# A kernel of local and full attention: Exp planned at another rate, LayerNorm scalars on other engines, final checks in another place

## The chip, the cores and the metric

The kernel runs on one core of one Trainium2 chip. The metric is the device time of one execution in microseconds (us), read as the median of several executions. The profile comes from one of these executions (for the kernel before, from a further one of 1501.95 us), with its own span and its own mean granted clock of TensorE. Engines are named as in the profile: PE is TensorE (PEld its weight loads), DVE VectorE, ACT ScalarE, POOL GpSimd, SP SyncE. A reading "L1481" is a line of the kernel. Before and after have different line numbers for the same code; where both matter, both are given.

## The reference

Four residual layers on a bf16 array x of 2048 rows and 512 columns: local attention A, full attention B, then A and B again with the same weights. Both have 32 heads of width 16. A lets each row look at 8 rows before it at a step of 2. B shares one key and one value head among all query heads.

```python
# cut to what matters
def _layernorm(x, eps=1e-5):
    return (x - mean(x)) / sqrt(var(x) + eps)

def _B_ref(x, wq, wk, wv, wo):            # S = 2048, H = 32, Dh = 16
    q = (x @ wq).reshape(B, S, H, Dh).transpose(0, 2, 1, 3)
    k, v = x @ wk, x @ wv
    p = softmax(einsum("bhqd,bkd->bhqk", q, k) * Dh ** -0.5)
    return merge_heads(einsum("bhqk,bkd->bhqd", p, v)) @ wo

x = A_x
x = x + _A_ref(_layernorm(x), A_wqkv, A_wo)
x = x + _B_ref(_layernorm(x), B_wq, B_wk, B_wv, B_wo)
x = x + _A_ref(_layernorm(x), A_wqkv, A_wo)      # the same two again
x = x + _B_ref(_layernorm(x), B_wq, B_wk, B_wv, B_wo)
```

B sets the time: two layers with 2048 x 2048 scores for 32 heads make 4096 tiles of 128 keys by 512 queries, and each needs an exponential.

## The kernel before

The program has a scheduler of its own. When the kernel is built, it plays all work through with a planned duration for each operation and fixes the order of instructions on each engine. On the chip the order is never changed: each engine takes its instructions in turn and waits on semaphores. The plan's constants (biases, priorities) were searched for a short plan.

A score tile takes one of two ways. Two tiles go through an Exp on ScalarE, or one tile goes through a copy on VectorE that writes an integer from which an integer addition (the "pass", on VectorE and on GpSimd) makes the bits of an exponential.

```python
# planned durations: the Exp of n tiles, in the scheduler
    def exp(self, s, _):
        ...
        t = 426.7 * n + 52                    # 905 ns for two tiles
        S.run("act", s, t)
        done = s + t + LAT["act"]
        ...

# what it emits
    def exp(self, key, slot, pt, n):          # ScalarE: two tiles
        self.chain("act", self.nc.scalar.activation(out=self.pt[pt][:, 0:n, :], in_=..., func=AF.Exp, scale=E_SCALE))
    def copy(self, bank, buf, r):             # VectorE: one tile
        self.chain("dve", self.nc.vector.tensor_scalar(out=self.t[buf][:, r, :].bitcast(I16), in0=self.dv[bank][:],
                                                       scalar1=-U_BIAS, scalar2=U_BIAS, op0=ALU.max, op1=ALU.add))
    def do_pass(self, e, buf, out, j, n, both):
        if e == "pool":                       # int32 add on GpSimd, 1.9 us
            ...
        else:                                 # int16 add on VectorE
            ...

# LayerNorm: statistics on VectorE, four small GpSimd operations, then four norms on whichever engine is free
        def scalars(op, some):
            g, x = nc.gpsimd, slice(some[0], some[-1] + 1)
            self.chain("pool", g.tensor_scalar_add(out=ve[:, x], in0=mv[:, x, 1], scalar1=EPS))
            self.chain("pool", g.tensor_tensor(out=rstd[:, x], in0=ve[:, x], in1=self.w.nhalf[:, x], op=ALU.pow))
            self.chain("pool", g.tensor_tensor(out=nmr[:, x], in0=mv[:, x, 0], in1=rstd[:, x], op=ALU.mult))
            self.chain("pool", g.tensor_scalar(out=nmr[:, x], in0=nmr[:, x], scalar1=-1.0, scalar2=None, op0=ALU.mult))
        ...
            def norm(op, i=i, xn=xn):
                if op.eng == "act":
                    k = nc.scalar.activation(out=xn.t[:], in_=src(i), func=AF.Identity, scale=rstd[:, i:i + 1],
                                             bias=nmr[:, i:i + 1])
                else:
                    k = self.pick(op).tensor_scalar(out=xn.t[:], in0=src(i), scalar1=rstd[:, i:i + 1],
                                                    scalar2=nmr[:, i:i + 1], op0=ALU.mult, op1=ALU.add)
            n = xn.used(sm.used(self.op({"act": 830.0, "dve": 690.0, "pool": 940.0}, 0, norm, [nm[i], *xn.prev],
                                        prio=322.6 + self.PRIO, port=("pool",))))
```

`port` names the engines for which the scheduler keeps an operation off the VectorE passes and GpSimd passes that run at that time.

At the end, VectorE compares all sums and reciprocals of the softmax with limits ("flags"), reduces them to a minimum, and a tiny matmul counts the partitions that passed.

## Time and profile before

| | before |
|---|---|
| median of 3 runs | 1503.88 us (1503.73 to 1510.52) |
| span of the profiled run, granted clock | 1500.2 us, 0.994 |
| busy PE, DVE, ACT, POOL | 95%, 89%, 96%, 60% |
| Exps, VectorE copies | 1359, 1378 |
| idle ACT, DVE | 63 us, 161 us |

Lines of a group read: line, engine, operation, output<-input with shapes, count | busy us, mean ns of one record | idle time of the engine just before them and what ended it. The prediction shows the lines that bear on the bound. Three more are needed later. The first is the page's chain of waits by engine: the work that ended last, followed back to what each step waited for, as shares of the span. The second is the table of 50 us windows, here the one from 150 to 200 us, where the loss will show (columns: length; busy us of PE, PEld, DVE, ACT, POOL with counts; clock; DMA share; GB/s). The third is the view of one tile, the normed rows, on VectorE (count: shortest/median/longest ns, first and last start):

```profile
ACT 45%; PE 42%; issue 7%; DVE 4%; POOL 1%; DMA 0%; ACTq 0%; POOLq 0%; DVEq 0%
```

```profile
150.00:200.00 50.00, 48.63 (x391) 15.61 (x393) 41.02 (x74) 45.98 (x55) 25.99 (x21) 1.00 0.11 22
```

### The profile page before, as it was taken

Reading aid. Unit: us, or ns where it says so; the run is one execution under the profiler, and the core shown is the slowest. Engines: PE = TensorE matmul, PEld = TensorE weight load, DVE = VectorE, ACT = ScalarE, POOL = GpSimd, SP = SyncE. Lnnn points to the kernel's source line nnn. Section 1 sums busy time; section 2 is a strip of 40 time slices with the busy share of each in tenths; the row PEclk is TensorE's granted clock in tenths of the full one; section 3 lists DMA queues with packets and bytes.
Section 4 is the critical chain, followed back from the end, with each engine's and each line's share of the span. In section 5 each row is a group of like instructions: output and inputs, shape, how many; then the busy total and the mean of one; then the engine's idle time right before and its main releaser. Section 6 shows DMA issues by size and latency. Waiting matters only on the chain.

```text
span 1500.2 us, 42220 instructions
## 1 busy us (share of the span) xinstructions
PE 1430.8 (95%) x17204; PEld 494.9 (33%) x17263; DVE 1339.5 (89%) x2301; ACT 1437.1 (96%) x1754; POOL 896.9 (60%) x741
## 2 busy tenths in 40 slices
PE   8899999999999999999999999999999999999996
PEld 4534343223422233222333224322222222222222
DVE  5787868998799978999789997899999999999997
ACT  6899999999999999999999999999999999999995
POOL 3745546565566656666575664757566656665664
PEclk9999999999999999999999999999999999999999
DMA  4010110011010020100201001001000000000000
GB/s 142 5 29 3 30 16 16 17 31 34 14 23 13 17 38 7 27 13 16 35 13 27 13 15 16 16 9 43 27 12 14 13 23 17 9 18 20 16 9 24
DMA packets 84114, 32.95 MB, mean 22 GB/s; under 512 B 71688, under 2 KB 77448, under 8 KB 83912
## 3 DMA queue, kind: packets, MB, share of 16 engines
q1 hardware_dynamic: 83048, 28.33, 8.8%
q8 instruction: 137, 2.24, 0.6%
q10 hardware_dynamic: 864, 1.84, 0.3%
q14 instruction: 65, 0.53, 0.1%
HBM read 13.53 MB, written 2.61 MB: 11 GB/s over the span
## 4 chain that ended last, share of the span: by engine, by line
ACT 45%; PE 42%; issue 7%; DVE 4%; POOL 1%; DMA 0%; ACTq 0%; POOLq 0%; DVEq 0%
ACT pt L1481 40%; PE o L1507 14%; PE st L1466 14%; PE y L1130 3%; ACT P L1353 2%; PE q L1130 2%; PE k L1130 2%; PE qb L1130 2%; DVE t L1485 2%; PE v L1297 1%; PE dv L1466 1%; ACT logs L1403 1%; ACT rec L1405 1%; PE st L1346 1%; DVE i L1495 1%
## 5 line engine op out<-in xcount | busy, mean ns | idle before, releaser
L1481 ACT ACTIVATE pt<-st 128x1024 bf16<-128x1024 f32 x1359 | 1271.8, 1168 | 16.9 <-PE o L1507 9.1
L1490 POOL TENSOR_TENSOR i<-t,off 128x1024 int32<-128x1024 int32 x345 | 656.2, 1904 | 488.1 <-DVE i L1495 332.7
L1485 DVE TENSOR_SCALAR t<-dv 128x512 int16<-128x512 f32 x1378 | 877.9, 683 | 51.3 <-PE dv L1466 41.5
L1466 PE MATMUL st<-QT,KAB 32*128 32x512 bf16 x1388 | 270.4, 381 | 13.4 <-ACT pt L1481 8.1
L1466 PE MATMUL st<-QT,region 32*128 32x512 bf16 x1330 | 259.1, 379 | 18.4 <-ACT pt L1481 13.9
L1507 PE MATMUL o<-pt,region 128*32 128x512 bf16 x1330 | 270.7, 386 | 0.2
L1507 PE MATMUL o<-i,region 128*32 128x512 f16 x1436 | 265.3, 385 | 1.0 <-DVE i L1495 0.7
L1507 PE MATMUL o<-pt,VEa 128*32 128x512 bf16 x1388 | 261.0, 386 | 0.4 <-DVE x_sb L1429 0.4
L1495 DVE TENSOR_SCALAR i<-t 128x2048 int16<-128x2048 int16 x345 | 238.6, 695 | 3.9 <-PE o L1507 3.1
L1507 PE MATMUL o<-i,VEd 128*32 128x512 f16 x1320 | 240.4, 385 | 0.8 <-POOL i L1490 0.7
L1466 PE MATMUL dv<-QT,region 32*128 32x512 bf16 x718 | 231.5, 382 | 1.0 <-DVE t L1485 1.0
L1466 PE MATMUL dv<-QT,KAB 32*128 32x512 bf16 x660 | 214.6, 383 | 0.0
L1507 PE MATMUL o<-t,region 128*32 128x512 f16 x718 | 181.5, 385 | 0.2 <-DVE t L1485 0.2
L1466 PEld LDWEIGHTS <-region 32*128 32x128 bf16 x2048 | 95.5, 90 | 259.6 <-issue 255.2
L1466 PEld LDWEIGHTS <-KAB 32*128 32x128 bf16 x2048 | 90.7, 90 | 264.4 <-issue 258.0
L1507 PE MATMUL o<-t,VEd 128*32 128x512 f16 x660 | 173.7, 385 | 0.6 <-issue 0.6
L1507 PEld LDWEIGHTS <-region 128*32 128x32 f16 (+1 forms) x3484 | 73.8, 94 | 162.4 <-issue 158.3
L1353 ACT ACTIVATE P<-st 128x576 bf16<-128x576 f32 (+1 forms) x128 | 89.6, 726 | 3.4 <-PE st L1346 3.3
L1507 PEld LDWEIGHTS <-VEd 128*32 128x32 f16 x1980 | 64.4, 94 | 72.6 <-issue 67.7
L1507 PEld LDWEIGHTS <-VEa 128*32 128x32 bf16 x1388 | 58.1, 94 | 79.6 <-issue 77.7
L1360 DVE TENSOR_TENSOR P<-P,bandmask 128x576 int32<-128x576 int32 x64 | 59.0, 926 | 28.3 <-ACT P L1353 26.1
L1414 POOL TENSOR_TENSOR logs<-logs 128x256 f32<-128x256 f32 x64 | 47.5, 742 | 30.2 <-ACT rec L1405 30.2
(173 smaller groups left out, 1180.3 us busy)
## 6 DMA issues: line engine op xcount, KB each, us to landing
lb<-rd SPq DMA_DIRECT2D x31, 256.0 KB
X<-X SPq DMA_DIRECT2D x124, 32.0 KB
k<-oncA SPq DMA_DIRECT2D x48, 64.0 KB
w_sb<-in_A_wqkv_dram ACTq DMA_DIRECT2D x4, 384.0 KB
region<-in_A_x_dram SPq DMA_DIRECT2D x3, 512.0 KB
out_dram<-w_sb SPq DMA_DIRECT2D x3, 512.0 KB
S<-X SPq DMA_DIRECT2D x62, 8.0 KB
rd<-R SPq DMA_DIRECT2D x62, 8.0 KB
```

The source lines that it names most:

```text
L1130: self.chain("pe", self.nc.tensor.matmul(st["ps"][:], lhsT=lhsT, rhs=rhs, start=first and n == 0, stop=last and n == len(some) - 1))
L1297: self.chain("pe", nc.tensor.matmul(ps[0][64 * a:64 * a + 64, i], lhsT=B.xnT.t[:, kt, kb * 64:(kb + 1) * 64], rhs=wv[:, kt, a, :, :], star ...
L1346: self.chain("pe", nc.tensor.matmul(st[:, j, col:col + w], lhsT=kx[gs], rhs=qt[gs, qbase + q0:qbase + q0 + w], start=True, stop=True, tile ...
L1353: "act", nc.scalar.activation(out=P.t[:, gh, :, c0:UC], in_=self.st.pop(sc)[:, :, c0:UC], func=AF.Exp, scale=DH ** -0.5)), [sc], frees=[sc ...
L1360: self.chain("dve", nc.vector.tensor_tensor(out=x, in0=x, in1=self.w.band[:].unsqueeze(1).to_broadcast([128, 16, NQ // 2]), op=ALU.bitwise ...
L1414: self.chain("pool", nc.gpsimd.tensor_tensor(out=lg.t[:], in0=lg.t[:], in1=lg.t[:], op=ALU.mult))
L1466: self.chain("pe", self.nc.tensor.matmul(out, lhsT=self.KAB[l][32 * g:32 * g + 32, a, kt * 128:(kt + 1) * 128], rhs=self.QT[32 * g:32 * g ...
L1481: self.chain("act", self.nc.scalar.activation(out=self.pt[pt][:, 0:n, :], in_=self.st.pop(key)[:, 0:n, :], func=AF.Exp, scale=E_SCALE))
L1485: self.chain("dve", self.nc.vector.tensor_scalar(out=self.t[buf][:, r, :].bitcast(I16), in0=self.dv[bank][:], scalar1=-U_BIAS, scalar2=U_B ...
L1490: i = self.nc.gpsimd.tensor_tensor(out=self.i[out][:, 0:n, :].bitcast(I32), in0=self.t[buf][:, 0:n, :].bitcast(I32), in1=self.w.off[j][:, ...
L1495: i = self.nc.vector.tensor_scalar(out=self.i[out][:, 0:n, :].bitcast(I16), in0=self.t[buf][:, 0:n, :].bitcast(I16), scalar1=J_OFF[j], sca ...
L1507: self.chain("pe", self.nc.tensor.matmul(self.o[bank][32 * g:32 * g + 32, :], lhsT=lhsT, rhs=rhs, start=first, stop=last, tile_position=(0 ...
```

## The change

The intent: plan Exp at the rate at which it was seen to complete (916 ns for two tiles in place of 905), so that the plan fits the chip better; take the slow GpSimd operations out of the LayerNorm that stands at the very start; move the checks out of the tail; let ScalarE take the first evacuation of an output block. Then the scheduler's constants were searched anew, some 40 of them.

```diff
-        t = 426.7 * n + 52
+        t = 426.7 * n + 63
...
+            if quick:                          # the first two chunks of layer 0
+                for eng, t, fn in (("act", 60.0, log), ("act", 60.0, power), ("dve", 70.0, shift)):
+                    ag = sm.used(self.op(eng, t, ...))     # Ln, Exp(-0.5 x), one multiply by -mean
+            else:
+                ag = sm.used(self.op("pool", 1700.0, lambda op, some=some: scalars(op, some), [ag], prio=2859.4 + self.PRIO))
...
-        e = X.used(self.op("dve", 599.0, evac, ...))
+        e = X.used(self.op({"act": act_ns(512), "dve": 599.0} if fresh else {"dve": 599.0}, 0, evac, ...))
...
-        self.op("dve", 2300.0, most, [evac, *self.seen, *sees], prio=LATER)      # flags and minimum in one block in the tail
+            small = self.op("dve", 560.0, ...)   # flags and minima in pieces, most of them among the stream,
+            wide = [self.op("dve", 410.0, ...)]  # the last ones ahead of the four final additions
...
-    BIAS = {"act": -50.0, "act2": 1946.7, ..., "lag": -1045.1, "both": 216.8, "next": 634.6, ...}
+    BIAS = {"act": -73.0, "act2": 1096.6, ..., "lag": -2342.9, "both": -263.5, "next": 869.6, ...}
-            n = ...(norm, prio=322.6 + self.PRIO, port=("pool",))
+            n = ...(norm, prio=329.3 + self.PRIO, port=("pool",))
```

## The prediction

> **What bounds the kernel now.** I read the page first, then a table of 50 us windows, the groups by line, the waits, and at last the timeline of both ends. The page's first part:
>
> ```profile
> PE 1430.8 (95%) x17204; PEld 494.9 (33%) x17263; DVE 1339.5 (89%) x2301; ACT 1437.1 (96%) x1754; POOL 896.9 (60%) x741
> ```
>
> PE looks as full as ACT, but its matmuls are pipelined and four small ones overlap, so the waits decide between them (us in total, times, longest):
>
> ```profile
> DVE t L1485 <- PE dv L1466: 41.5, 77, 3.3
> ...
> PE st L1466 <- ACT pt L1481: 22.0, 102, 0.5
> ...
> ACT pt L1481 <- PE o L1507: 9.1, 14, 1.3
> ```
>
> TensorE's score matmuls wait for ScalarE's Exp 102 times; the Exp (L1481) hardly waits. The windows (PE, PEld, DVE, ACT, POOL busy with counts; clock; DMA share; GB/s) say where:
>
> ```profile
> 0.00:50.00 50.00, 43.09 (x787) 25.35 (x795) 30.14 (x85) 34.63 (x64) 22.47 (x63) 1.00 0.34 108
> 50.00:100.00 50.00, 45.66 (x897) 21.76 (x893) 39.84 (x82) 42.86 (x73) 31.87 (x50) 0.93 0.06 13
> ...
> 900.00:950.00 50.00, 48.49 (x988) 21.49 (x988) 37.90 (x61) 48.46 (x73) 25.50 (x22) 1.00 0.10 13
> ...
> 1100.00:1150.00 50.00, 47.72 (x475) 14.38 (x473) 49.33 (x84) 50.00 (x56) 31.51 (x19) 1.00 0.05 12
> ...
> 1450.00:1500.00 50.00, 38.36 (x328) 12.48 (x326) 39.41 (x66) 33.79 (x41) 25.25 (x17) 0.94 0.07 22
> ```
>
> ScalarE idles 15.4 + 7.1 us in the first 100 us, 16.2 us in the last 50, and only about 24 us in the 27 windows between. **ScalarE is the bound**, and where pure attention runs (1100 to 1150) VectorE is full beside it; VectorE has room only where the local-attention layer runs (900 to 950: 12 us idle). Total idle: ScalarE 63 us, VectorE 160 us. What fills them:
>
> ```profile
> L1481 ACT ACTIVATE pt<-st 128x1024 bf16<-128x1024 f32 x1359 | 1271.8, 1168 | 16.9 <-PE o L1507 9.1
> ...
> L1485 DVE TENSOR_SCALAR t<-dv 128x512 int16<-128x512 f32 x1378 | 877.9, 683 | 51.3 <-PE dv L1466 41.5
> ```
>
> From the start times, an Exp that is never held starts 904 to 906 ns after the last one (678 of 1359), and one in a full stretch with a late plan 915 to 918 (56 Exps in 51.7 us from 1099: (51.7 - 1.3)/55 = 0.916). 905 is what the scheduler plans now (426.7*2 + 52), 916 what it will plan (+63). All starts together lose 43 us against 905 each; the 547 Exps spaced 906 to 930 ns lose only 7 of them, 115 gaps of more than 950 ns lose 33.
>
> **What the Trainium skill says.** "ScalarE: Activation LUTs", section What ACT_TABLE_LOAD costs: an ACTIVATE takes 186 ns + 0.833 ns per column, each pointer operand adds 93 ns, and neighbours overlap by 93. For 1024 columns that is a spacing of 946 ns; this trace shows 905 to 916, so I use the trace and keep the page only for the new two-column Ln and Exp, which no trace has yet. Same page, section Table sets: one set holds both ln and exp. The trace agrees: Ln (L1403) and Exp (L1405) alternate 64 times with one table load of 1283 ns in the run, so the new Ln costs no load. "GPSIMD Engine Reference", section 3.1: a GpSimd instruction pays two software dispatch hops. Agrees: operations on two columns take 206 to 278 ns there, the power 715. "Perfetto Trace Analysis", section on the DVE / Act instruction: a record runs until the write is acknowledged, so neighbours overlap; agrees (mean 1168 ns at a spacing near 0.91 us). So durations must not be added up; I use spacings.
>
> **The change part by part**, from the instruction order of both programs and this trace's spacings.
>
> (a) *Fewer Exps.* 1359 become 1350 of full size and one half: -9 x 0.905 + 0.48 = -7.7 us of ScalarE. 17 tiles go to VectorE: +17 copies x 0.598 and +4 integer passes x 0.598 = +12.6 us.
>
> (b) *Other ScalarE work moves.* Plain casts and copies change by +3 in sum (fresh X evacuations +6, which may now run on ScalarE; QT +5; q +2; oncA -6; v -4): +1.4 us at 0.47. Masked k +2, kb -1: +0.6 us at 0.57. One norm less: -0.75. Four tiny VEa/VEd evacuations more: +0.4 at 0.104. Eight Ln and eight Exp of two columns: by the page 0.28 and 0.19 us less the overlap, an estimate of 0.15 each: +2.4. ScalarE's work in sum: -7.7 + 1.4 + 0.6 - 0.75 + 0.4 + 2.4 = **-3.7 us**. VectorE gains some 15 us (the 12.6, seven more norms, oncA +6, less what left), into 160 us of idle time.
>
> (c) *The start.* LN's chain for the first two tiles now:
>
> ```profile
> 7.51 0.24 POOL L1161 TENSOR_SCALAR sm<-sm 128x2 f32<-128x2 f32 x1 [3.19 <-DVE sm L1157]
> 7.84 0.73 POOL L1162 TENSOR_TENSOR sm<-sm,nhalf 128x2 f32<-128x2 f32 x1
> ...
> 8.65 0.20 POOL L1163 TENSOR_TENSOR sm<-sm 128x2 f32<-128x2 f32 x1
> 8.93 0.23 POOL L1164 TENSOR_SCALAR sm<-sm 128x2 f32<-128x2 f32 x1
> 9.20 0.81 ACT L1179 ACTIVATE xn<-region,sm 128x512 bf16<-128x512 bf16 x1 [5.15 <-POOL sm L1164]
> ```
>
> 1.69 us. Ln 0.28, Exp 0.19, one VectorE operation 0.17 (as the two-column kscale) and three hops of 0.05 to 0.09 make about 0.85: 0.84 us less. The second pair also waited behind a norm on GpSimd (10.12 against an aggregate ready at 8.83), so the first q matmul should come at 12.5 instead of 14.02. The weights are no limit: their queue is empty by 9 us. The same chain before the first Exp at 77.3 gives some 0.8 more, and the tiny operations that stand in ScalarE's full queue are already counted in (b). I take **-2.3 us**.
>
> (d) *The end.* VectorE's last work now (start, us, what):
>
> ```profile
> 1487.26 0.76 DVE w_sb L1652 x2
> 1488.02 1.05 DVE i L864 x5
> ...
> 1489.10 1.56 DVE chk_mb L868
> 1490.65 2.38 DVE w_sb L1623 x4
> 1493.04 0.35 DVE i L872
> ```
>
> Flags and minimum over all sums (2.6 us) stand before the four last additions, and flag, minimum, count and compare after them, until 1494.5; then 5.7 us of branch and close. In the new order most flags move in among the stream's copies, and flag and minimum of the last reciprocals stand before the additions (1.05 us), beside the last output matmuls, which end at 1489.96 anyway. The additions can start near 1489.3 and end at 1491.7, the compare at 1491.9: **-2.6 us**. The last X copy goes to ScalarE, which is neutral.
>
> (e) *Gaps.* A plan with the true rate should leave fewer gaps; of the 33 us I give it 3, as every bias was tuned again and I can't tell what that does: **-3 +/- 7 us**.
>
> Sum: -3.7 - 2.3 - 2.6 - 3 = -11.6 us. 1503.9 - 11.6 = **1492.3 us**.
>
> **The rivals.** *VectorE takes over as the bound*: in 1100 to 1150 it runs a group of five operations in 3.01 us, at 0.598 each that is full. If the 17 tiles land there, they add up to 12.6 us to VectorE and cancel (a): about 1500. Against it speak its idle 160 us and the waits on dv (41.5 us). *TensorE's order hides the correction*: Exps are fed in a fixed order through two slots, and 102 waits of PE for pt say that the spacing of 0.916 is a closed loop of both; then a plan at 916 changes nothing by itself, and only ends and tile split remain: about 1495. *The new plan closes most gaps*: the 33 us fall by half, and the time goes to about 1480. *The start is hidden*: ScalarE has work waiting from 19 us on, so an earlier start could be eaten; costs 2 us.
>
> **Range and chances.** The parts that I can count give 1494 to 1497; gaps add the spread. Range 1481 to 1502. Over 2% faster would need 1474, which takes nearly all gaps: 4%. Over 2% slower needs VectorE or a broken order to cost 40 us: 1%.
>
> **What would show it.** Right: 1351 Exps and 1395 copies; ScalarE's idle time in the first 100 us down by about 2; last compare within 4 us of the last reciprocal multiply at the end; the 100 to 1450 windows with ScalarE's idle sum below 24 us; the pure stretches still at 50.00 of 50. Wrong: DVE windows at 50 while ACT falls below 49 (first rival); waits of ACT for PE above 20 us; an end that is not shorter. My number fails if the retuned biases move gaps by more than 10 us either way.

## More of the kernel before

```profile
L1182 DVE TENSOR_SCALAR xn<-x_sb,sm x7: 536/643/2173, 82.8 to 888.6; 128x512 bf16<-128x512 f32 x7
```

ScalarE is busy 46 of 50 us there at full clock. VectorE does 7 norms of f32 rows, the typical one in 0.64 us, one in 2.17.

## The result, and the profile after

| | before | after |
|---|---|---|
| median | 1503.88 us | 1509.74 us (1506.58 to 1511.01, 5 runs) |
| ratio | | 1.0025, interval 1.0001 to 1.005 |
| profiled span, clock | 1500.2 us, 0.994 | 1508.0 us, 0.991 |
| Exps, copies | 1359, 1378 | 1351, 1395 |
| excess of the Exp spacings: from each Exp's start to ScalarE's next start, less 905 ns, summed | 43.1 us | 57.5 us |
| TensorE at half clock, from its first full clock to 1480 us | 10.2 us | 23.9 us |

The change made the kernel a little slower, 1509.7 in place of the predicted 1492.3.

The page of the kernel after, its busy shares, its chain of waits and the two ways of a tile:

```profile
PE 1451.0 (96%) x17258; PEld 485.0 (32%) x17316; DVE 1361.6 (90%) x2332; ACT 1438.8 (95%) x1769; POOL 887.4 (59%) x707
...
PE 47%; ACT 31%; DVE 15%; issue 6%; POOL 1%; DMA 0%; ACTq 0%; DVEq 0%; POOLq 0%
...
L1492 ACT ACTIVATE pt<-st 128x1024 bf16<-128x1024 f32 x1351 | 1264.5, 1141 | 24.0 <-PE dv L1477 9.3
...
L1496 DVE TENSOR_SCALAR t<-dv 128x512 int16<-128x512 f32 x1395 | 881.8, 681 | 32.1 <-PE dv L1477 26.5
```

ScalarE's busy time hardly moved (1437.1 to 1438.8), but its idle time grew by 6 us, and its Exp now waits 24.0 us in place of 16.9. Between 100 and 1450 us it idles 34.5 us in place of 24.2. In the chain that ended last, ScalarE fell from 45% to 31% and VectorE rose from 4% to 15%.

The waits of the kernel after (us in total, times, longest):

```profile
DVE t L1496 <- PE dv L1477: 26.5, 48, 2.6
...
ACT pt L1492 <- PE dv L1477: 9.3, 24, 1.1
...
PE st L1477 <- ACT pt L1492: 7.8, 36, 0.5
```

TensorE waits for an Exp 36 times where it did so 102 times before. ScalarE is now the one that waits.

Where it goes, by windows of the kernel after:

```profile
100.00:150.00 50.00, 47.74 (x908) 20.62 (x910) 37.12 (x58) 46.77 (x71) 25.54 (x25) 0.90 0.07 13
150.00:200.00 50.00, 47.82 (x358) 13.44 (x359) 39.79 (x67) 42.92 (x52) 23.61 (x19) 0.86 0.12 22
...
1100.00:1150.00 50.00, 49.77 (x484) 14.10 (x482) 49.96 (x85) 50.00 (x55) 32.49 (x20) 1.00 0.04 10
```

From 150 to 200 us ScalarE loses 3.1 us against before, at a clock of 0.86. Counting tiles as they start (two for an Exp, one for a copy) gives the same picture: both kernels have started 68 tiles at 110 us; at 190 us it is 249 before and 224 after; at 1450 us 3995 and 3968. **In this pair of traces nearly the whole lag arises between 110 and 190 us; later it swings from 17 to 33 tiles and ends at 27.** In pure attention the two are level. The experiments will show that what is repaired there and what is repaired by freeing the norms are not the same.

What VectorE did there is in the chain of waits of that stretch (share of its 12 us by line; start, us, what):

```profile
by line: DVE t L1496 44.6%; DVE xn L1193 15.2%; DVE sm L1147 10.0%; PE dv L1477 5.4%; DVE x_sb L1440 5.3%; DVE X L1537 5.1%; DVE i L1506 5.0%; PE o L1518 4.5%; PE o L1071 4.0%; PE st L1477 3.0%; DVE sm L1153 2.2%; issue 0.5%
...
155.48 1.82 DVE xn L1193
157.31 2.39 DVE t L1496 x4
```

And this is the timeline of the kernel after at that place, first GpSimd, then TensorE (start, us, what):

```profile
155.13 1.89 POOL L1501 TENSOR_TENSOR i<-t,off 128x1024 int32<-128x1024 int32 x1
```

```profile
157.96 0.37 PE L1477 MATMUL dv<-QT,KAB 32*128 32x512 bf16 x1 [1.07 <-DVE t L1496]
```

A norm on VectorE took 1.9 us here, not 0.6. A GpSimd pass ran from 155.13 to 157.02, and the norm ended at 157.30. The copies behind it came late, and TensorE stood still for 1.07 us. This is not the only one. The view of the normed rows on VectorE, in the kernel after:

```profile
L1193 DVE TENSOR_SCALAR xn<-x_sb,sm x11: 535/1373/2170, 78.3 to 975.0; 128x512 bf16<-128x512 f32 x11
```

Eight of these norms took 1.07 to 2.17 us, and **each of the eight ended 0.28 or 0.29 us after the end of a GpSimd pass that ran beside it.** Against 0.55 us each that is about 9.5 us of VectorE. Before, three were held, for some 2.4 us in sum. The new constants had sent more norms to VectorE (11 of f32 rows in place of 7), and the plan counted 0.69 for each.

The Trainium skill has this: "SBUF — State Buffer", section Who interferes with whom, says that VectorE's second port pair is GpSimd's as well, that an operation in a 2-port mode needs it (`tensor_scalar` can enter one), and that whichever of the two starts first holds it for its whole instruction. The trace agrees in that all eight norms end just behind the pass. In six of them the pass had started 0.04 to 1.11 us before the norm; in the other two both records start within 0.001 us, so these don't show who was first.

Right after the held norm TensorE's clock falls. Windows of 3.41 us of the kernel after, cut at the change of the clock:

```profile
156.79:160.20 3.41, 2.22 (x19) 0.44 (x17) 3.41 (x6) 2.82 (x4) 2.89 (x5) 0.99 0.28 58
160.20:163.61 3.41, 3.30 (x23) 0.70 (x25) 3.41 (x7) 2.70 (x4) 1.31 (x2) 0.50 0.59 99
163.61:167.02 3.41, 3.41 (x25) 0.58 (x18) 2.08 (x4) 2.43 (x3) 3.41 (x3) 0.50 0.00 0
```

TensorE was busy 2.22 of 3.41 us, and then ran at half clock until 173.8. "TensorE: Matmul & The Clock Gate", Part 1 of the Trainium skill, tells of a monitor that halves TensorE's clock after an idle window of about 3.4 us, in windows that don't start with the kernel. Every half-clock stretch before the end of these traces lasts one to four times 3.41 us, so that agrees; but no window had to be idle, as this one shows.

The end of the kernel after, for step (d) (start, us, what):

```profile
1497.99 0.42 DVE L864 TENSOR_SCALAR xnT<-lb 128x512 bf16<-128x512 f32 x1
1498.45 0.69 DVE L867 TENSOR_REDUCE chk_mb<-xnT 128x1 bf16<-128x513 bf16 x1
1499.40 0.69 DVE L1637 TENSOR_TENSOR w_sb<-x_sb,y 128x512 bf16<-128x512 f32 x1 [0.26 <-PE y L1716]
1500.05 1.88 DVE L1637 TENSOR_TENSOR w_sb<-x_sb,st 128x512 bf16<-128x512 f32 x3
1501.85 0.14 DVE L874 TENSOR_SCALAR chk_bad<-chk_cnt 1x1 int32<-1x1 f32 x1
```

From the last evacuation of an output block to the end of the span it is 13.2 us, before 15.6.

### The profile page after: what moved, and what is told of

Its sections match the earlier page's. It is cut to its first block, busy times and chain, and to the rows that moved or that the text cites. A ratio compares the mean times of both kernels' runs of the same rounds, so it can differ in the third digit from the quotient of the medians. Undisturbed runs are those within 1.5% of the kernel's fastest.

```text
span 1508.0 us, 42381 instructions
## 1 busy us (share of the span) xinstructions
PE 1451.0 (96%) x17258; PEld 485.0 (32%) x17316; DVE 1361.6 (90%) x2332; ACT 1438.8 (95%) x1769; POOL 887.4 (59%) x707
## 4 chain that ended last, share of the span: by engine, by line
PE 47%; ACT 31%; DVE 15%; issue 6%; POOL 1%; DMA 0%; ACTq 0%; DVEq 0%; POOLq 0%
ACT pt L1492 26%; PE o L1518 17%; PE st L1477 15%; DVE t L1496 8%; PE y L1126 3%; ACT P L1364 2%; PE dv L1477 2%; DVE i L1506 2%; PE k L1126 2%; PE q L1126 2%; PE qb L1126 2%; PE v L1308 2%; ACT logs L1414 1%; ACT rec L1416 1%; PE st L1357 1%
## 5 line engine op out<-in xcount | busy, mean ns | idle before, releaser
L1501 POOL TENSOR_TENSOR i<-t,off 128x1024 int32<-128x1024 int32 (+1 forms) x349 | 661.7, 1897 | 483.5 <-DVE i L1506 317.9
L1518 PE MATMUL o<-i,VEd 128*32 128x512 f16 x1348 | 245.3, 389 | 0.3 <-POOL i L1501 0.2
L1477 PE MATMUL dv<-QT,region 32*128 32x512 bf16 x721 | 240.5, 381 | 2.9 <-DVE t L1496 2.7
L1506 DVE TENSOR_SCALAR i<-t 128x2048 int16<-128x2048 int16 (+1 forms) x349 | 242.5, 696 | 0.4
L1477 PE MATMUL dv<-QT,KAB 32*128 32x512 bf16 x674 | 219.9, 384 | 4.2 <-DVE t L1496 3.7
L1518 PE MATMUL o<-t,region 128*32 128x512 f16 x721 | 186.8, 385 | 0.0
L1477 PEld LDWEIGHTS <-KAB 32*128 32x128 bf16 x2048 | 85.3, 91 | 258.3 <-issue 253.7
L1477 PEld LDWEIGHTS <-region 32*128 32x128 bf16 x2048 | 85.1, 90 | 239.4 <-issue 236.6
L1518 PEld LDWEIGHTS <-region 128*32 128x32 f16 (+1 forms) x3490 | 77.9, 93 | 190.5 <-issue 183.9
```

The lines of the kernel that those rows point to most:

```text
L1477: self.chain("pe", self.nc.tensor.matmul(out, lhsT=self.KAB[l][32 * g:32 * g + 32, a, kt * 128:(kt + 1) * 128], rhs=self.QT[32 * g:32 * g ...
L1501: i = self.nc.gpsimd.tensor_tensor(out=self.i[out][:, 0:n, :].bitcast(I32), in0=self.t[buf][:, 0:n, :].bitcast(I32), in1=self.w.off[j][:, ...
L1506: i = self.nc.vector.tensor_scalar(out=self.i[out][:, 0:n, :].bitcast(I16), in0=self.t[buf][:, 0:n, :].bitcast(I16), scalar1=J_OFF[j], sca ...
L1518: self.chain("pe", self.nc.tensor.matmul(self.o[bank][32 * g:32 * g + 32, :], lhsT=lhsT, rhs=rhs, start=first, stop=last, tile_position=(0 ...
```

## The experiments

Three theories stood at first. **Plan:** Exp on this chip starts 904 to 905 ns after the last one whenever it is fed, in the kernel after too (760 of 1351), so a plan at 916 puts 11 ns x 1351 = 14.9 us of lateness into the order; the excess over 905 grew by 14.4 us. The traces say what the 916 is: in the kernel before, nine in ten of the 360 Exps that start 914 to 919 ns after another start about 0.10 us after the end of the last score matmul, so they waited for TensorE; of the 614 that start 903 to 906 ns after another, 95% start later than that after it, most by 0.12 to 0.35 us. **Clock:** the loss is the 13.7 us more at half clock. **Scatter:** any new order moves the time by some us. The held norm came as a fourth from the second set of traces.

How much the clock moves a single run is seen without any change: 43 runs of the kernel before, made beside the experiments, lie between 1499.18 us (clock 0.997) and 1510.63 (0.986), with a slope of 1.08 us for 0.001 of clock and a correlation of -0.96. So 3 us at half clock go with about 1 us of time. The ratios below are each to the kernel before in the same rounds on one chip, and a difference of 2 us is at the edge of what they can tell. The kernel after was not run again beside the experiments: where one is compared with it, two ratios of different rounds are compared, and the intervals of both count.

### More idle matmuls everywhere (stir95_after, stir95_before)

```diff
-SPAN, ACTIVE = 3413.0, 0.74
+SPAN, ACTIVE = 3413.0, 0.95
```

The scheduler puts in matmuls of a zero tile where it plans TensorE idle. More of them, all else in the same order.

> The kernel after with 93 more idle TensorE matmuls of a zero tile (186 more rows with their weight loads), put in where the scheduler thinks TensorE would otherwise stand still; the order of all other instructions on all engines is unchanged. Clock theory: the loss of 20 to 25 tiles between 115 and 190 us comes from the half-speed TensorE clock that the trace of after shows at 122.8-129.6, 136.4-139.8 and 160.3-174.0 us (23.9 us, against 10.2 us before); the half-clock stretches after 115 us go away, the tiles done at 190 us return to within 8 of the 249 of before, and the time falls by 5 to 9 us to 1501-1505. Plan theory (the order with Exp planned at 916 ns starves ScalarE by itself): the half-clock stretches may go, but the time stays at 1507-1511 and the deficit at 190 us stays over 18 tiles.

> The control of the above: the kernel before with 94 more idle TensorE matmuls and nothing else moved. Clock theory: it has only 3.4 us at half clock after the start (114.8-118.2), so it gains 0 to 2 us: 1502-1504. Plan theory: 1503-1505. If the idle matmuls get in the way of real ones, both kernels lose the same few us.

Measured: after 1508.16 us (ratio to before 1.0019, 0.999 to 1.0048), before 1505.48 (1.0012, 0.9976 to 1.0049). The stretches at 122 and 136 us went away in the kernel after, but one from 157.9 to 171.6 stayed: between 150 and 162 us the scheduler put in no more idle matmuls than before, as its plan sees no idle time there. So this tested the clock theory only in part, and its expectation of 1501 to 1505 missed. The control didn't move.

### The planned rate alone (noR_after905, onlyR_before916)

```diff
 # noR_after905: the kernel after with        # onlyR_before916: the kernel before with
-        t = 426.7 * n + 63                     -        t = 426.7 * n + 52
+        t = 426.7 * n + 52                     +        t = 426.7 * n + 63
```

> The kernel after with Exp planned at 905 ns again (52 in place of 63 of fixed cost), all else of the change kept; the scheduler lays a new order. Plan theory: the 11 ns times 1351 Exps are 14.9 us of lateness that the plan itself puts in, and the excess of Exp's spacing over 905 ns falls from 57.5 to about 43 us; time 1495-1502. Clock theory: the time goes only with the half-clock sum of the run (half of it in us added). Scatter theory (every new order moves the time by 5 to 10 us whatever was altered): anything from 1500 to 1520, with the Exp excess unrelated to the planned rate.

> The kernel before with Exp planned at 916 ns and nothing else of the change. Plan theory: time rises by 10 to 15 us to 1514-1519 and the Exp excess over 905 ns rises from 43 to 55-60 us. The theory of the prediction (the rate only trades a few Exps for copies): within 4 us of 1504. Scatter theory: a move of 5 to 10 us in either direction without a change of the Exp excess by the planned 15 us.

Measured: after with 905 1513.04 us (1.0044, 1.0014 to 1.0073), before with 916 1510.63 (1.0034, 1.0008 to 1.006). The excess of the Exp spacings moved the way the plan theory said, but by less: 57.5 to 49.4 (43 expected) and 43.1 to 54.4 us (55 to 60). The time followed it in one of the two only: the kernel before lost 5 us with 916, but going back to 905 made the kernel after slower, with 9 Exps more and a busy time of ScalarE of 1446.2 us. Both orders were new and their constants searched for another one. So the rate decides how closely Exps follow each other, and fewer Exps pay for a part of it; it isn't the cause by itself. ScalarE's share of the chain of waits follows the planned rate too, whatever the time: it is 44% in noR_after905, the slower kernel, and 39% in onlyR_before916.

### Which engine sets the pace (expcut, copycut)

```diff
 # expcut: Exp of 32 columns fewer              # copycut: copy of 32 columns fewer
-  out=pt[:, 0:512*n], in_=st[:, 0:512*n]       -  out=t[:, 0:512], in0=dv[:, 0:512]
+  out=pt[:, 0:512*n-32], in_=st[:, 0:512*n-32] +  out=t[:, 0:480], in0=dv[:, 0:480]
```

(Written on flattened tiles; the result is wrong, the order is unchanged on every engine.)

> Wrong result on purpose. The kernel after, same order on every engine, with each Exp writing 32 columns fewer of its last tile: from the page's own slope (905 ns for 1024 columns, of which 427 per 512 in the plan) some 27 ns less each, 36 us less of ScalarE work in sum. If ScalarE paces the kernel after everywhere: the time falls by about 36 us to 1473. If the order paces it (a late fill for TensorE or VectorE before each Exp), ScalarE only waits longer: a fall of under 15 us, and the starts of Exps stay 930 ns apart on average where they were.

> Wrong result on purpose. The same cut on the kernel before (1359 Exps, 36 us). Theory that the plan at 905 keeps ScalarE fed and bound: it falls by more than the kernel after does, 25 us or over, to 1479 or less. If the closed loop through TensorE and the two Exp slots paces both kernels: both fall alike and by under 15 us.

> Wrong result on purpose. The kernel after, same order, each VectorE score copy 32 columns fewer: some 33 ns each by the plan's slope, 46 us less of VectorE work. If VectorE has become a bound through the 17 tiles more (DVE 15% of the chain in place of 4%): the time falls by 8 us or more to below 1502. If VectorE has room and only follows the order: within 3 us of 1509.

> Wrong result on purpose. The same cut on the kernel before: VectorE was 4% of its chain, so it should gain 0 to 4 us (1500-1504); a gain as large as that of the kernel after would say that the VectorE share of the chain did not grow through the change.

Measured, two runs each: expcut before 1482.12 us (0.9867, 0.9839 to 0.9896), expcut after 1503.29 (1.0008, 0.9957 to 1.0059); copycut before 1504.91 (1.0019), copycut after 1507.40 (1.0035). Some 36 us less of ScalarE's work brought the kernel before 20 us and the kernel after 3 by the ratios, 6 by the medians. So more than half of what ScalarE saved came back in the kernel before, and little in the kernel after: **ScalarE paced the kernel before, and paces the kernel after much less.** The chain of waits of the kernel after with the shorter Exp:

```profile
PE 50%; DVE 31%; ACT 12%; issue 5%; POOL 1%; DMA 1%; ACTq 0%; DVEq 0%; POOLq 0%; SPq 0%
```

VectorE and TensorE hold it. But shorter copies showed no gain either, in either kernel, which speaks against the mass of VectorE's work. Two runs tell little, though: both of copycut_after had a clock of 0.989, against 0.991 to 0.994 of the kernel after, and by the slope above some 3 us of gain could hide in that (an estimate). In both cut kernels with the order of after, a norm at 155 and 157 us still took 1.9 and 2.0 us, and the half clock still began, at 160.4 and 161.7. That pointed from the engine to the order.

### The held norm and the clock dip, apart and together (noport_after, fill_after, both_after), and the tail alone (onlyC_before)

```diff
 # noport: the VectorE norm writes out its accumulator too; order unchanged
-                    k = self.pick(op).tensor_scalar(out=xn.t[:], ..., op0=ALU.mult, op1=ALU.add)
+                    more = dict(accum_out=self.w.acc[:]) if op.eng == "dve" else {}
+                    k = self.pick(op).tensor_scalar(out=xn.t[:], ..., op0=ALU.mult, op1=ALU.add, **more)
 # fill: 13 matmuls of a zero tile between 152 and 161 us, in TensorE's order alone
+        if self.mode is not None and self.end >= self.fill_at and any(a <= self.end < b for a, b in FILL):
+            more = self.stir(self.mode, self.end, [512])
 # onlyC: the kernel before with the new tail, nothing else
```

The skill's page on SBUF, cited above, excepts from the 2-port modes the form of `tensor_scalar` that also writes out its accumulator.

> The kernel after, same order of all instructions on all engines; only the VectorE norms (17, of which 11 on f32 rows) also write out their accumulator to an unused column, the form that by the Trainium skill takes no 2-port mode. Theory of the held port: in the trace of after 8 of the VectorE norms took 1.07 to 2.17 us where they take 0.54 to 0.61 unhindered, each ending 0.2 to 0.3 us after a GpSimd pass that was running; the norms then take 0.6 to 0.8 us each (about 9 us of VectorE time back), the TensorE dip at 154-160 us (2.2 of 3.4 us busy) and the half-clock stretch at 160-174 after it go away, and the time falls by 3 to 7 us to 1502-1506. Rival: VectorE has 10% room and the norms are only 17; the norms get short but the time stays within 2 us of 1509.

> The kernel after with 13 idle matmuls of the zero tile (512 columns, some 0.2 us each) put into TensorE's order between about 152 and 161 us, where TensorE was busy only 2.79 and 2.22 of two 3.4 us windows; all else unchanged, the held norm too. Clock theory: the half-clock stretch at 160-174 us is gone, the tiles done at 190 us rise from 224 to 234 or more, and the time falls by 3 to 6 us. Rival (the loss there comes from waits on VectorE, the clock only shows them): the stretch may go, but the tiles at 190 us stay below 229 and the time within 2 us of 1509.

> Both of the above at once. If the held port causes the dip and the dip causes the half clock, the two are one chain: the gain is that of the larger of the two plus at most 2 us, 1501-1505. If they are two independent losses, the gains add up to 8 us or more.

> The kernel before with the new tail alone (flags moved in among the stream, last minimum ahead of the output additions). Step (d) of the prediction: the last X evacuation to the end of the span falls from 15.6 us to about 13.2, as the trace of after shows, and the time by 2.4 us, 1501-1502.5. Rival: the flags moved into the stream cost VectorE what they free at the end: within 1 us of the kernel before.

| | median | ratio to before | interval |
|---|---|---|---|
| noport_after | 1500.28 us | 0.9976 | 0.9959 to 0.9993 |
| fill_after | 1505.51 us | 1.0008 | 0.9994 to 1.0022 |
| both_after | 1499.25 us | 0.9974 | 0.9959 to 0.9989 |
| onlyC_before | 1501.12 us | 0.9981 | 0.9965 to 0.9997 |

The kernel after stood at 1.0025. With nothing changed but the form of 17 VectorE norms it falls by 0.49%, 7 us, below the kernel before; by the two intervals it can be 3 to 12 us. The clock isn't the reason: at 0.991 the kernel after took 1509.7 to 1511.0 us and noport_after 1504.2 and 1504.5, at 0.992 1507.9 and 1500.9, at 0.994 1506.6 and 1499.7. The result turned out wrong (relative error 0.065); what the form does to it was not looked into. The order and the shapes are what is timed, and noport_before below, wrong through the same edit, is the control for the form. The same view of noport_after:

```profile
L1194 DVE TENSOR_SCALAR_CACHE_REDUCE xn<-x_sb,sm x11: 790/797/805, 81.4 to 970.2; 128x512 bf16<-128x512 f32 x11
```

All eleven take 0.80 us; an unhindered one took 0.54. None is held, though the GpSimd passes still run beside them.

Thirteen idle matmuls at the dip, with the norm still held, go with 2.6 us less (1.0025 to 1.0008; the medians differ by 4.2), which the two intervals don't separate from nothing. The windows of fill_after at the same place:

```profile
156.79:160.20 3.41, 3.29 (x29) 1.12 (x29) 3.41 (x7) 3.08 (x4) 2.39 (x4) 1.00 0.49 81
160.20:163.61 3.41, 3.41 (x39) 0.90 (x36) 3.41 (x7) 3.41 (x5) 1.81 (x1) 1.00 0.38 75
```

TensorE is busy 3.29 of 3.41, and the stretch at half clock doesn't come; ScalarE is busy 3.41 of the next window in place of 2.70. So filling the dip takes this stretch away: it stood at 158 to 162 us in all five profiled runs of this order without the filling, and in neither of the two with it.

Is it one chain, from the held norm to the idle TensorE to the half clock? Both edits together give 0.9974, hardly more than the norm alone, which would fit a chain, but the intervals don't exclude that the gains add up. The trace of noport_after speaks against it: with the norm free the half clock still came, from 161.9 to 172.1, after this window:

```profile
158.50:161.91 3.41, 2.82 (x25) 0.81 (x23) 3.41 (x6) 3.41 (x5) 3.22 (x5) 0.99 0.48 79
```

The tiles say where each edit wins (one trace each; tiles started, two for an Exp, one for a copy):

| | tiles by 190 us | tiles from 110 to 190 us | half clock there | tiles from 190 to 1450 us | half clock there |
|---|---|---|---|---|---|
| before | 249 | 181 | 3.4 us | 3746 | 0 |
| after | 224 | 156 | 23.9 us | 3744 | 0 |
| noport_after | 225 | 166 | 13.7 us | 3759 | 0 |
| fill_after | 237 | 169 | 6.8 us | 3737 | 17.1 us |
| both_after | 240 | 178 | 0 | 3769 | 0 |

From 110 to 190 us the tiles follow the half clock, whether the norm is held or not; fill_after reaches the 234 tiles at 190 us that were expected. Freeing the norms shows itself after 190 us, where seven of the eight were held: 15 tiles more than the kernel after and 13 more than the kernel before, at full clock in all three. So **these traces show two losses: TensorE's half clock goes with most of the lag that is seen at 190 us, and the held norms take away, bit by bit, what the new order would win later.** That a held norm starts a half-clock stretch is not shown. In the chain of waits of noport_after ScalarE has 37% and VectorE 9%, in place of 31% and 15%.

The tail alone brought 2.3 us by the medians, as step (d) had it, and its trace has 12.9 us from the last evacuation to the end. But its runs had a better clock (mean 0.9956) than the kernel before in the same rounds (0.9925), which by the slope would be worth 3 us; at a clock of 0.994 it took 1503.3 and 1503.9 us, the kernel before 1502.4. The shorter tail is seen; a gain in time isn't.

### The rest: the same edit on before, the LN split alone, and new searches (noport_before, onlyL_before, port905, port916, free905, port905_again)

```diff
 # noport_before: the edit of noport_after on the kernel before
 # onlyL_before: the kernel before with the LN split alone
 # port905, port916: the kernel after with 905 or 916, its constants searched afresh, and
-                                        prio=329.3 + self.PRIO, port=("pool",))))
+                                        prio=..., port=("pool", "dve"))))
 # free905: as port905, searched alike, with port=("pool",) kept
```

The searches were for a short plan, without a chip.

> Wrong result on purpose[...], same order. The edit of noport_after on the kernel before, whose 9 VectorE norms lost only about 2.5 us behind GpSimd passes (two of 0.92 us, one of 2.17 us). If held norms set the two kernels apart: a gain of 0 to 3 us, so that it ends level with noport_after (1500.3) or above it. If the edit makes any order faster (for example by taking some other stop away): a gain of 6 us or more, as in the kernel after (9 us).

> The kernel before with the LN scalars of the first two chunks on ScalarE and VectorE and nothing else; the scheduler lays a new order. Prediction's step (c): first q matmul at 12.5-12.9 us in place of 14.0, the first Exp 2 us earlier than 77.3, time 2.3 us less (1501-1502). Rival: the start's gain is eaten before 50 us and the new order moves the rest: first q at 12.9, first score matmuls of the second chunk (49.8 us) within 0.5 us of before, time anywhere from 1500 to 1513.

> Candidate: all code of the change, Exp planned at 905 ns, the scheduler told that VectorE norms keep off running GpSimd passes too, and its constants searched afresh. Expected: no VectorE norm over 1 us, tail 13 us, Exp excess over 905 below 45 us, time 1493-1500, below both kernels. If the norms were only a small part and the result is scatter of orders: 1500-1510.

> The same with Exp planned at 916 ns, its constants searched from those of the kernel after. If the rate of 916 costs by itself what it plans (up to 15 us less what the search regains): 1500-1508 and an Exp excess of 50 us or more, at least 5 us over port905. If the rate is neutral once the norms are free: within 3 us of port905.

> Control for port905: the same code of the change, Exp at 905 ns, constants searched with the same effort to the same planned length (0.13 us shorter), but the scheduler not told of the port; it puts 16 norms on VectorE where port905 puts 3. If the port matters: several of these norms take 1 to 2.2 us, TensorE is at half clock for longer than in port905, and the time is 4 us or more above port905, 1499-1506. If only the new search counts: within 2 us of port905.

> The kernel port905 once more, beside its control: 1495 within 2 us, and 5 to 9 us below the kernel before on this chip.

| | median | ratio to before | interval |
|---|---|---|---|
| noport_before | 1503.76 us | 0.9995 | 0.9971 to 1.0019 |
| onlyL_before | 1515.23 us | 1.0081 | 1.0056 to 1.0105 |
| port905 | 1495.35 us | 0.9949 | 0.9928 to 0.9971 |
| port916 | 1497.81 us | 0.9961 | 0.9939 to 0.9983 |
| free905 | 1499.75 us | 0.9971 | 0.9947 to 0.9995 |
| port905_again | 1496.37 us | 0.9956 | 0.9930 to 0.9981 |

The edit that brought the kernel after 7 us brings the kernel before nothing. So it isn't a faster form in general. The three norms that were held there, for 2.4 us in sum, are too few to show in an interval of this width.

The LN split alone laid an order that is 12 us slower. Its first q matmul came at 12.9 us (14.0 before), its first score matmul of the second chunk at 49.7 (49.8): **the start's gain was gone by 50 us**, as in the kernel after (12.9, then 50.1). The 12 us come from the rest of the order, and they show how far constants that were found for another program can be off; where they arise was not followed up.

The two kernels whose scheduler knows of the port are the fastest of all with the right result, by the ratios 6 to 8 us below before and 10 to 11 below after. In the trace of port905 VectorE has three norms, none of f32 rows (the view of one tile):

```profile
L1193 DVE TENSOR_SCALAR xn<-region,sm x3: 411/412/413, 10.8 to 81.3; 128x512 bf16<-128x512 bf16 x3
```

and its chain of waits, by engine, is again that of the kernel before, as in all kernels planned at 905 with whole Exps (42 to 45% for ScalarE, the slow onlyL_before included), so it is no sign of speed:

```profile
ACT 45%; PE 44%; issue 6%; DVE 4%; POOL 1%; ACTq 0%; DVEq 0%; POOLq 0%
```

Its profiled run has no half-clock stretch at all before the end (clock 0.998), its second one three (0.994). The control free905 puts 16 norms on VectorE (its trace names 15), of which seven took 0.94 to 1.87 us, and is 3.4 us above port905_again by the medians, 0.15% by the ratios; the intervals overlap. So the new search is the larger part of what port905 gains, and the port's own part there is likely but not separated. The rate of 916 costs 2.5 us by the medians against 905 in this pair, and the intervals overlap too; port916's profiled run was at a clock of 0.986, so its Exp excess (49.3 us against 41.7) can't be laid to the rate alone.

## Why the prediction was wrong

**Step (a), fewer Exps:** right. 1351 in place of 1359, 17 copies more.

**Step (b), other work moves:** this is the step that failed. The prediction counted "seven more norms" to VectorE as part of 15 us "into 160 us of idle time", and took sums where order counts. The norms went to VectorE at places where GpSimd ran passes, and eight of them took 1.07 to 2.17 us. Taken away by itself, this is 7.4 us (1.0025 to 0.9976 of 1503.9 us; 5 to 7 at the same clock), of the 15.4 us between the predicted gain of 11.6 and the loss of 3.8 that the ratio shows. It is enough to turn the loss against the kernel before into a gain. The rival "VectorE takes over as the bound" looked for 12.6 us more work in the pure stretches; VectorE is full there (49.96 of 50), and the time wasn't lost there.

**Step (c), the start:** the shorter path came as said, 12.88 us for the first q matmul against the predicted 12.5. But the gain is 0 by 50 us, and the first Exp of full attention came at 80.2 in place of 77.3; at 110 us the two kernels are level in tiles. Up to that Exp ScalarE runs 128 operations in place of 108, 16 of them the new Ln and Exp (0.30 and 0.21 us each in the trace); why it comes later is not settled. ScalarE's idle time in the first 100 us did fall, from 22.5 to 19.9 us, as the prediction asked, but with those operations in it. The rival "the start is hidden" fits the traces; the 2.3 us are then lost in full.

**Step (d), the end:** right in the trace, 2.4 us shorter against the predicted 2.6. That the time gets it was not seen.

**Step (e), gaps:** predicted at -3 with a band of 7, measured at +14.4; ScalarE's idle time from 100 to 1450 us rose from 24.2 to 34.5 us, where the prediction's own sign of being right was less than 24. Of the 14.4, 8.5 go with the norms alone (noport_after: an excess of 49.0 us, with the same 23.9 us at half clock as the kernel after). The other 5.9 would fit the rate: at the same code the excess grew by 8 and by 11 us from 905 to 916 in two pairs, about what the fewer Exps save. That is argued, as every pair has two orders. The sentence that failed is "A plan with the true rate should leave fewer gaps". 916 was not Exp's rate. It was the spacing of Exps that waited for TensorE's last matmul; fed in time, an Exp starts after 904 to 905 in both kernels. The second rival, "TensorE's order hides the correction", named this closed loop and was not given its weight.

**Not in the prediction at all:** TensorE's clock. The half-clock time before the end more than doubled in the profiled run, and the lag at 190 us follows it. What it costs in the end was not measured: the 2.6 us that go with filling one dip lie within the noise. Over the runs the kernel after had a mean clock of 0.992, about that of the kernel before (0.992 to 0.994).

Of the 15.4 us, then, some 5 to 7 are shown by an experiment on an unchanged order and 2.3 are read from traces; the rest lies in the gaps that go with the rate, in the clock and in what the new constants did, and no run separates these.

## What to carry to other kernels

In a kernel with a fixed order, a planned duration is a decision about order. A spacing read from a stretch in which the engine waited is no property of the instruction, and should not go into the plan. Before a plan moves small work to an engine "with room", look at what else holds that engine's shared port at that time, and at what waits behind it; a median far above the shortest record of the same instruction is the sign. When a repair works, look in its trace for the place where it wins: here it was not the place where the lag had been seen. Where the time of one kernel varies, put the granted clock beside each run before comparing.

## What the Trainium skill lacked or had wrong

- "TensorE: Matmul & The Clock Gate", Part 1, speaks of an idle window before the half clock and of one busy window, about 3.4 us, after which the full clock returns. Here a window with 2.22 of 3.41 us busy was followed by 13.7 us at half clock, with TensorE busy for 3.30 to 3.41 us of each of the four windows in it. In all 20 traces (up to 1480 us), 58 of 67 half-clock starts followed a window busy for less than 88%, but some 400 such windows, down to 63%, went by without one, so a share of busy time isn't the rule. The page has no threshold for a window that is partly busy.
- "SBUF — State Buffer", Who interferes with whom, is right about the held port. Elsewhere the page gives the wait of a transfer behind a VectorE operation; for a VectorE norm behind a GpSimd addition the wait ended 0.28 to 0.29 us after the GpSimd record (8 of 8). It doesn't say what the accumulator form costs: 0.80 us against 0.54 for 512 columns of f32 to bf16, and 0.08 us to read the accumulator, nor whether the output stays the same; here the result was wrong by 0.065.
- "ScalarE: Activation LUTs", What ACT_TABLE_LOAD costs, leads to a spacing of 946 ns for 1024 columns; the median here is 904 ns in the kernel after.
